# A Fourier-mixing and gated-MLP layer on one core: the first eight chunks alternate real and imaginary matrix, and four x tiles are normed on VectorE

## The chip, the core and the metric

One core of a Trainium2 chip runs the whole program in one launch. It has TensorE (PE: matmuls, with weight loads listed as PEld), VectorE (DVE), ScalarE (ACT), GpSimd (POOL) and SyncE (SP), which here only issues transfers. Each engine works through its own list of instructions strictly in the order in which the program wrote them, and waits on semaphores for the others. The metric is the time of one execution in microseconds (us). The kernel before takes 949.74 us, the median of three runs (949.63 to 949.95).

## The reference, cut to what matters

```
mod = (silu(c) @ w_mod).reshape(6, 512)      # sa, ca, ga, sb, cb, gb
h = layernorm(x) * (1 + ca) + sa             # x: 2048 x 512
a, b = h @ hid_re.T, h @ hid_im.T
x = x + ga * (seq_re @ a - seq_im @ b)       # seq_re, seq_im: 2048 x 2048
h = layernorm(x) * (1 + cb) + sb
z = gelu(h @ w_in)                           # 512 x 1792
z1, z2 = z[:, :896], layernorm(z[:, 896:])
x = x + gb * ((z1 * (w_sp @ z2 + b_sp)) @ w_out)
```

The change touches the front of the first Fourier part alone: the layernorm of x, and the products of the two 2048x2048 sequence matrices with it.

## The kernel before, in words

The kernel computes the Fourier part as (sequence matrix @ normed x) @ hidden matrix. All products are made from split operands: a number is cut into a high part in the fp32r type and a low part that holds the rest, and each product is three matmuls, high times high, high times low and low times high (`matmul3`, L93 to L97; `mm_a`, L425, for the first chunks). One matmul has a 128x128 stationary operand and a 128x512 moving one.

The sequence matrices are read in quarters of 512 output rows (t = 0 to 3). For a quarter, a **block** is 512x512 of the real matrix `cr` (j = 0) or the imaginary `ci` (j = 1), 1 MB, loaded by four transfers into a `stage` tile (L151 to L165; two such buffers). A block gives four **chunks** n: 128 columns of the block, transposed by DVE into half of a `t` tile (L176 one chunk, L216 two at once), high part `ah` on ACT (L245), low part `al` on DVE (L252). Chunk n is multiplied with tile s of the normed x: four groups of 128 hidden columns, twelve matmuls a chunk. There are four `ah` buffers, three `al` buffers and two `t` pairs, so a chunk can be made ready only a few chunks ahead of PE. For t = 0 the blocks come as cr, ci for rows of x 0 to 511, then cr, ci for the next 512, and so on: chunks 0 to 3 use cr with x tiles 0 to 3, chunks 4 to 7 use ci with the same tiles, chunks 8 to 11 use cr with x tiles 4 to 7.

An x tile is 128 rows. Its path is: statistics on DVE (`stats_first` L367 for tiles 0 to 3, `stats_x` L364 with L103 and L105 for 4 to 9), mean and 1/sqrt on POOL (L374 and L375, or L107, L108 and L115), normed tile `xn` on ACT (L119), high part `hh` on ACT (L412), low part `hl` on DVE (L417). Tiles 0 to 3 are loaded at the start, 64 KB or 128 KB a transfer, between the pieces of the first block; of block 0 the first 64 columns of each 128 come first. Each transfer is issued by SP or ACT, and eight completion semaphores go round: a transfer can be issued only when the eighth before it has landed.

The order is written out by hand. `at(n, f, ...)` puts a step behind chunk n's matmuls, and `prep(n)` runs ahead of them: it makes the low part of chunk n+2, the transposition of n+4 and n+5 and the high part of n+3. The lists at L897 to L949 set the steps for the start and for x tiles 4 to 15. Four throwaway matmuls (L329 to L333) stand at the front of PE's list.

Of the kernel before, what the change touches and what calls it, by code (L numbers as in the profile page):

```python
# [8 lines left out]
F32 = mybir.dt.float32  # L9
F32R = mybir.dt.float32r  # L10
# [9 lines left out]
def fnet_gmlp_kernel(  # L20
# [102 lines left out]
    def at(n, f, *a):  # L123
        fill.setdefault(n, []).append((f, a))
# [50 lines left out]
    def squares(dst, block, k):  # L175
        nc.vector.transpose(dst.rearrange("p (b i) -> p b i", i=32), block[:, :, 32 * k:32 * k + 32])  # L176
# [173 lines left out]
    def load_x(g, ks=range(4), engs=(nc.sync,)):  # L350

        if g not in XG:
            if g % 2:
                XG[g] = spool.tile([P, 4, D], F32, tag="x", bufs=1, name=f"x{g}")
            else:
                XG[g] = hpool.tile([P, 4, D], F32, tag="h12", bufs=1, name=f"x{g}")
        k0, k1 = ks[0], ks[-1] + 1
        v = x.rearrange("(g a k i) d -> g a i k d", g=NQ, a=4, i=32)
        for a in range(4):
            engs[a % len(engs)].dma_start(XG[g][32 * a:32 * a + 32, k0:k1, :], v[g, a][:, k0:k1, :])  # L360
        for k in ks:
            X[4 * g + k] = XG[g][:, k, :]
# [4 lines left out]
    def stats_first(s):  # L367

        m = spool.tile([P, 12], F32, tag="first", bufs=4, name=f"first{s}")
        nc.vector.bn_stats(m[:, :6], X[s])  # L370
# [53 lines left out]

    def mm_a(n):  # L425
        t, r = divmod(n, 8 * NQ)
        j, s = ((r // 4) % 2, r // 8 * 4 + r % 4) if t == 0 else (r // NS, r % NS)
        if s == 0:
            for k in range(ND):
                GP[t, j, k] = bank(4 * j + k if t == 0 else ring[0] % 6, f"gp{t}_{j}_{k}")  # L430
                ring[0] += t > 0
        ah, al = AH.pop(n), AL.pop(n)
        if n < 4:
            order = (h_hi[s], al), (h_lo[s], ah)
            for a, b in ((h_hi[s], ah),) + (order if n else order[::-1]):
                for k in range(ND):
                    nc.tensor.matmul(GP[0, 0, k], a[:, k, :], b, start=s == 0 and b is ah and a is h_hi[s], stop=False)
# [446 lines left out]


    both = (nc.sync, nc.scalar)
    load_x(0, range(1), both)
    stage[0] = blocks.tile([P, 16, P], F32, tag="stage", bufs=2, name="stage0")
    load_block(stage[0], src[0], 0, P // 2, both)
    load_x(0, range(1, 2), both)  # L890
    nc.scalar.activation(sc, ones[:, :ND], AF.Silu)
    load_x(0, range(2, 4))
    load_block(stage[0], src[0], P // 2, P)
    load(1)
    load_x(1, range(2))
    keep_busy(4, 5)
    for s in range(4):  # L897
        LN[s] = spool.tile([P, D], F32, tag="xn", bufs=4, name=f"xn{s}")
        nc.gpsimd.memset(LN[s][:, 0:1], 1.0)
    stats_first(0)  # L900
    norm_x(0)
    hi_h(0)
    turn_one(0)
    prep_hi(0, nc.vector)
    stats_first(1)
    lo_h(0)
    prep_lo(0)
    norm_x(1)
    hi_h(1)
    turn_one(1)  # L910
    prep_hi(1)
    stats_first(2)
    prep_lo(1)
    lo_h(1)
    norm_x(2)
    hi_h(2)
    turn_one(2)
    prep_hi(2)
    stats_first(3)
# [260 lines left out]
```

## Time and profile before

| what | value |
|---|---|
| median of three runs | 949.74 us |
| the profiled execution's own time | 950.4 us |
| its span on the core | 948.6 us |
| PE busy | 940.3 us (99%), 4160 matmuls |
| DVE busy | 704.5 us (74%) |
| ACT busy | 387.6 us (41%) |
| POOL busy | 175.5 us (19%) |
| granted TensorE clock, mean | 0.999 |
| moved by transfers | 161.25 MB, mean 170 GB/s |

A row of the timeline has the start in us from the start of the span, the duration in us, the engine, the line, the operation and the tiles that it writes and reads; "x4" merges four equal instructions, and the bracket names the idle time of the engine ahead of it and what ended it. A row of the waits has the total, the count and the longest. A row of the groups has the busy time and the mean duration in ns of one. A row of the windows has, for a stretch of the span, its length and each engine's busy time, then the granted clock, the share of the 16 transfer engines and the GB/s. The profile is one execution, 0.66 us above the median of the three runs.

### The profile page before, as it was taken

To read this page: it belongs to the slowest core of one execution; us is meant where nothing else is said; L and a number is where in the kernel's file an instruction comes from. 1 tells how busy PE (TensorE), PEld (TensorE's weight loads), DVE (VectorE), ACT (ScalarE), POOL (GpSimd) and SP (SyncE) were. 2 spreads that over 40 slices of the span, in tenths; PEclk is the share of its full clock that TensorE was granted. 3 is DMA by queue.
4 is the path that set the end of the run, shared out by engine and by line. 5 is a ranking of instruction groups with operands and counts; after the bars stand their busy time and mean duration, and the time that the engine had idled before them with its cause. 6 is when DMAs were issued, how large, how long until landed. Compare 5 with 4: busy or idle time off the path is not lost.

```text
span 948.6 us, 12279 instructions
## 1 busy us (share of the span) xinstructions
PE 940.3 (99%) x4160; PEld 780.9 (82%) x4160; DVE 704.5 (74%) x1039; ACT 387.6 (41%) x665; POOL 175.5 (19%) x331
## 2 busy tenths in 40 slices
PE   8999999999999999999999999999999999999998
PEld 5888888888888888888788999888888888888886
DVE  6799857775576666767978588877788688885872
ACT  4685424232132222322776456644544444331221
POOL 2431000121531144122432265200000000000000
PEclk9999999999999999999999999999999999999999
DMA  9997653676437965996596984555554455833551
GB/s 208 220 218 154 116 139 82 151 189 155 133 85 195 279 203 159 278 276 144 144 309 256 330 260 155 156 110 135 133 129 94 101 122 134 210 97 125 164 189 58
DMA packets 249230, 161.25 MB, mean 170 GB/s; under 512 B 130192, under 2 KB 218512, under 8 KB 249040
## 3 DMA queue, kind: packets, MB, share of 16 engines
q1 hardware_dynamic: 235792, 120.75, 52.8%
q0 software_dynamic: 11984, 39.07, 11.5%
q8 instruction: 32, 0.52, 0.2%
q10 hardware_dynamic: 1392, 0.66, 0.2%
q14 instruction: 30, 0.25, 0.1%
HBM read 123.73 MB, written 36.70 MB: 169 GB/s over the span
## 4 chain that ended last, share of the span: by engine, by line
PE 50%; DVE 1%; ACT 1%; POOL 1%; issue 0%; ACTq 0%; DVEq 0%; POOLq 0%
PE gw L96 10%; PE gw L95 10%; PE gw L97 10%; PE z2p L96 3%; PE z2p L97 3%; PE z2p L95 3%; PE op L97 3%; PE op L95 3%; PE op L96 3%; PE z1p L96 1%; PE z1p L95 1%; PE z1p L97 1%; PE z1g L95 1%; PE z1g L96 1%; PE z1g L97 1%
## 5 line engine op out<-in xcount | busy, mean ns | idle before, releaser
L245 ACT ACTIVATE ah<-t 128x512 fp32r<-128x512 f32 x263 | 164.4, 627 | 308.0 <-PE gp L97 183.3
L252 DVE TENSOR_TENSOR al<-t,ah 128x512 fp32r<-128x512 f32 x264 | 180.3, 686 | 141.7 <-PE gp L96 63.2
L96 PE MATMUL gp<-al,hh 128*128 128x512 f32 x496 | 193.1, 389 | 0.0
L95 PE MATMUL gp<-ah,hh 128*128 128x512 f32 x496 | 193.0, 389 | 0.0
L97 PE MATMUL gp<-ah,hl 128*128 128x512 f32 x496 | 193.0, 389 | 0.0
L97 PE MATMUL gw<-ah,bl 128*128 128x512 f32 x400 | 155.6, 389 | 0.0
L96 PE MATMUL gw<-al,bh 128*128 128x512 f32 x400 | 155.6, 389 | 0.0
L95 PE MATMUL gw<-ah,bh 128*128 128x512 f32 x400 | 155.6, 389 | 0.0
L96 PEld LDWEIGHTS gp<-al,hh 128*128 128x128 f32 x496 | 93.1, 188 | 19.7 <-DVE al L252 0.4
L95 PEld LDWEIGHTS gp<-ah,hh 128*128 128x128 f32 x496 | 93.1, 188 | 19.3
L97 PEld LDWEIGHTS gp<-ah,hl 128*128 128x128 f32 x496 | 93.1, 188 | 19.2
L97 PEld LDWEIGHTS gw<-ah,bl 128*128 128x128 f32 x400 | 75.1, 188 | 15.7
L95 PEld LDWEIGHTS gw<-ah,bh 128*128 128x128 f32 x400 | 75.1, 188 | 15.7
L96 PEld LDWEIGHTS gw<-al,bh 128*128 128x128 f32 x400 | 75.1, 188 | 15.4
L216 DVE STREAM_TRANSPOSE t<-stage 128x1024 f32<-128x1024 f32 x64 | 79.3, 1239 | 7.0 <-DMA stage<-in_A_dft_seq_re_dram 6.0
L210 DVE STREAM_TRANSPOSE t<-stage 128x1024 f32<-128x1024 f32 x56 | 69.4, 1239 | 0.1
L751 ACT ACTIVATE bh<-z 128x512 fp32r<-128x512 f32 (+1 forms) x56 | 32.8, 587 | 66.2 <-PE gw L96 66.2
L729 POOL DMA_DIRECT2D s_d<-sj x64 | 35.1, 550 | 109.2 <-DVE sj L721 64.7
L95 PE MATMUL yp<-hth,gh 128*128 128x512 f32 x128 | 49.8, 389 | 0.0
L96 PE MATMUL yp<-htl,gh 128*128 128x512 f32 x128 | 49.8, 389 | 0.0
L97 PE MATMUL yp<-hth,gl 128*128 128x512 f32 x128 | 49.8, 389 | 0.0
L96 PE MATMUL z2p<-wil,ah 128*128 128x448 f32 x128 | 46.7, 365 | 0.0
(204 smaller groups left out, 1420.4 us busy)
## 6 DMA issues: line engine op xcount, KB each, us to landing
stage<-in_A_dft_seq_im_dram SPq DMA_DIRECT2D x64, 256.0 KB, 5.6
sj<-in_B_w_sp_dram SPq DMA_DIRECT2D x32, 512.0 KB, 8.2
s_d<-sj POOLq DMA_DIRECT2D x64, 256.0 KB, 4.3
stage<-s_d SPq DMA_DIRECT2D x128, 128.0 KB, 2.8
stage<-in_A_dft_seq_re_dram SPq DMA_DIRECT2D x60, 256.0 KB, 5.4
stage<-in_B_w_sp_dram SPq DMA_DIRECT2D x96, 128.0 KB, 3.1
stage<-h_d SPq DMA_DIRECT2D x32, 256.0 KB, 6.2
wm<-in_w_mod_dram SPq DMA_DIRECT2D x16, 256.0 KB, 4.8
```

The costliest lines, as they stand in the source:

```text
L95: nc.tensor.matmul(acc, ah, bh, start=first, stop=False, skip_group_check=go_on)
L96: nc.tensor.matmul(acc, ah, bl, start=False, stop=False, skip_group_check=go_on)
L97: nc.tensor.matmul(acc, al, bh, start=False, stop=last, skip_group_check=go_on)
L210: nc.vector.transpose(t.rearrange("p r (b i) -> p r b i", i=32), st[:, :, :, 16 * k:16 * k + 32])
L216: nc.vector.transpose(t.rearrange("p k (b i) -> p k b i", i=32), st[:, :, 32 * k:32 * k + 64].rearrange("p b (k i) -> p k b i", k=2))
L245: nc.scalar.activation(AH[n], source(n), AF.Copy)
L252: nc.vector.tensor_tensor(AL[n], source(n), AH[n].bitcast(F32), op=ALU.subtract)
L729: nc.gpsimd.dma_start(s_d[m, r, g][b * P:(b + 1) * P, :], a)
L751: nc.scalar.activation(BH[p, k][:, :w], b_of(p, k), AF.Copy)
```

## The change

Five things change, all at the start.

1. Chunks 0 to 7 alternate: chunk n uses block n % 2 (cr or ci) and x tile n // 2. So x tile s serves chunks 2s and 2s + 1. `mm_a` writes all eight in the groups' order that only the first four had, and `turn_one` transposes one chunk at a time for all eight.
2. The loads at the front are reordered: x tile 0 in two transfers (SP and ACT) instead of four; then the first half of block 0 and the first half of block 1, each in four transfers by two issuers; then x tiles 1 and 2, the second halves of both blocks, x tile 3. Block 2 gets a buffer of its own (that of `wb`) and is loaded ahead of x tiles 4 to 7.
3. Rows 0 to 3 of x tiles (x tiles 0 to 3) are normed on DVE, (x - mean) * rstd in one tensor_scalar and a memset of one column (`norm_first`); POOL does one step (the power) instead of two, and ACT none.
4. Chunk 0 is transposed in two halves of 256; the high part of the first half is made by ACT, that of the second by DVE.
5. The steps for x tiles 4 and 5 are written into a new list: statistics of tile 4 behind chunk 4, its norm, high and low part and then the statistics of tile 5 behind chunk 5, and the rest of tile 5 behind chunk 6. Tiles 6 and up keep their places.

```diff
-    def turn_one(n):
-        squares(slot(n), stage[n // 4], n % 4)
+    def turn_one(n, b0=0, b1=16):
+        if b0 == 0:
+            slot(n)
+        squares(T[n][:, 32 * b0:32 * b1], stage[n % 2][:, b0:b1], n // 2)
...
-        nc.gpsimd.tensor_scalar(mv[:, 3:4], mv[:, 0:1], mv[:, 2:3], -1.0, op0=ALU.mult, op1=ALU.mult)
-        NRM[s] = mv[:, 2:3], mv[:, 3:4]
+        NRM[s] = mv[:, 0:1], mv[:, 2:3]
...
-        j, s = ((r // 4) % 2, r // 8 * 4 + r % 4) if t == 0 else (r // NS, r % NS)
+        j, s = (r % 2, r // 2) if n < 8 else ((r // 4) % 2, r // 8 * 4 + r % 4) if t == 0 else (r // NS, r % NS)
...
-        if n < 4:
+        if n < 8:
...
-            for a, b in ((h_hi[s], ah),) + (order if n else order[::-1]):
+            for a, b in ((h_hi[s], ah),) + (order if j == 0 else order[::-1]):
...
+    def load_row_tile(s):
+        v = x[:Q].rearrange("(a k i) d -> k a i d", a=4, i=32)[s]
+        for i in range(2 if s == 0 else 1):
+            o = slice(2 * i, 2 * i + 2) if s == 0 else slice(0, 4)
+            both[i].dma_start(XG[0][32 * o.start:32 * o.stop, s, :], v[o])
+    load_row_tile(0)
+    load_block(stage[0], src[0], 0, P // 2, both)
+    load_block(stage[1], src[1], 0, P // 2, both)
+    load_row_tile(1)
...
+    load_block(stage[2], src[2])
+    load_x(1, range(2))
...
+    def norm_first(s):
+        m = NRM.pop(s)
+        nc.vector.tensor_scalar(LN[s], X.pop(s), m[0], m[1], op0=ALU.subtract, op1=ALU.mult)
+        nc.vector.memset(LN[s][:, 0:1], 1.0)
...
+                     (4, (stats_x, 4), (prep_lo, 7), (turn_two, 8)),
+                     (5, (norm_x, 4), (hi_h, 4), (lo_h, 4), (stats_x, 5)),
+                     (6, (norm_x, 5), (hi_h, 5), (lo_h, 5))):
...
-    for s, n in ((4, 4), (5, 4), (6, 6), (7, 6), (8, 10), (9, 10)):
+    for s, n in ((6, 6), (7, 6), (8, 10), (9, 10)):
```

Line numbers of the changed kernel stand 7 higher from `turn_two` on, 6 higher behind `stats_first`, and 37 higher behind the start. Three places show how the instructions move.

DVE's list from the first statistics on, before (`first` holds an x tile's statistics, x0 the x tiles 0 to 3, t0 chunks 0 and 1):

```order
L370 BN_STATS first0_178<-x0_132 128x6
L372 BN_AGGR first0_178<-first0_178 128x2
L373 TENSOR_SCALAR first0_178<-first0_178 128x1
L176 STREAM_TRANSPOSE t0_187<-stage0_137 128x512
L243 TENSOR_SCALAR ah0_189<-t0_187 128x512
L370 BN_STATS first1_191<-x0_132 128x6
L372 BN_AGGR first1_191<-first1_191 128x2
L373 TENSOR_SCALAR first1_191<-first1_191 128x1
L417 TENSOR_TENSOR hl0_197<-xn0_170,hh0_185 128x512
```

And the same place now:

```order
L377 BN_STATS first0_172<-x0_134 128x6
L379 BN_AGGR first0_172<-first0_172 128x2
L380 TENSOR_SCALAR first0_172<-first0_172 128x1
L924 TENSOR_SCALAR xn0_177<-x0_134,first0_172 128x512
L925 MEMSET xn0_177 128x1
L176 STREAM_TRANSPOSE t0_182<-stage0_132 128x256 x2
L933 TENSOR_SCALAR ah0_184<-t0_182 128x256
L259 TENSOR_TENSOR al0_188<-t0_182,ah0_184 128x512
L423 TENSOR_TENSOR hl0_190<-xn0_177,hh0_180 128x512
```

The norm of tile 0 has come in ahead of the transposition, which is now two halves, and the statistics of tile 1 have gone behind both low parts and the transposition of chunk 1.

DVE's list around the work for chunks 8 and 9, before (bstx and mvx are statistics of x tiles 5, 6 and 7 in turn, x1 the x tiles 4 to 7, hl4 and hl5 the low parts of x tiles 4 and 5, al7 to al9 those of chunks 7 to 9):

```order
L103 BN_STATS bstx_364<-x1_160 128x6
L105 BN_AGGR mvx_366<-bstx_364 128x2
L252 TENSOR_TENSOR al7_373<-t6_288,ah7_332 128x512
L252 TENSOR_TENSOR al8_400<-t8_330,ah8_375 128x512
L216 STREAM_TRANSPOSE t10_402<-stage2_236 128x1024
L103 BN_STATS bstx_427<-x1_160 128x6
L105 BN_AGGR mvx_429<-bstx_427 128x2
L103 BN_STATS bstx_436<-x1_160 128x6
L105 BN_AGGR mvx_438<-bstx_436 128x2
L252 TENSOR_TENSOR al9_445<-t8_330,ah9_409 128x512
L417 TENSOR_TENSOR hl4_461<-xn4_394,hh4_423 128x512
L417 TENSOR_TENSOR hl5_463<-xn5_397,hh5_425 128x512
```

And the same place now (the statistics of tile 4 and al7 stand just ahead of it):

```order
L223 STREAM_TRANSPOSE t8_356<-stage2_157 128x1024
L423 TENSOR_TENSOR hl4_382<-xn4_377,hh4_380 128x512
L103 BN_STATS bstx_384<-x1_162 128x6
L105 BN_AGGR mvx_386<-bstx_384 128x2
L259 TENSOR_TENSOR al8_398<-t8_356,ah8_363 128x512
L223 STREAM_TRANSPOSE t10_400<-stage2_157 128x1024
L423 TENSOR_TENSOR hl5_426<-xn5_421,hh5_424 128x512
L103 BN_STATS bstx_428<-x1_162 128x6
L105 BN_AGGR mvx_430<-bstx_428 128x2
L103 BN_STATS bstx_437<-x1_162 128x6
L105 BN_AGGR mvx_439<-bstx_437 128x2
L259 TENSOR_TENSOR al9_446<-t8_356,ah9_407 128x512
```

The low parts hl4 and hl5, which stood behind all statistics of tiles 4 to 7 and behind al9, now stand ahead of the statistics of tile 5 and of tiles 6 and 7; al8 and al9 stand behind them.

SP's list of transfers from the start, before (stage0 is the first cr block, stage1 the first ci block, stage2 the second cr block; 32x16x64 is a quarter of half a block):

```order
L360 DMA x0_132<-in_A_x_dram 32x512 x2
L154 DMA stage0_137<-in_A_dft_seq_re_dram 32x16x64 x2
L360 DMA x0_132<-in_A_x_dram 32x512 x2
L360 DMA x0_132<-in_A_x_dram 32x2x512 x4
L154 DMA stage0_137<-in_A_dft_seq_re_dram 32x16x64 x4
L154 DMA stage1_155<-in_A_dft_seq_im_dram 32x16x128 x4
L360 DMA x1_160<-in_A_x_dram 32x2x512 x4
L154 DMA stage2_236<-in_A_dft_seq_re_dram 32x16x128 x4
L360 DMA x1_160<-in_A_x_dram 32x2x512 x4
```

And now:

```order
L901 DMA x0_134<-in_A_x_dram 64x1x512
L154 DMA stage0_132<-in_A_dft_seq_re_dram 32x16x64 x2
L154 DMA stage1_133<-in_A_dft_seq_im_dram 32x16x64 x2
L901 DMA x0_134<-in_A_x_dram 128x1x512 x2
L154 DMA stage0_132<-in_A_dft_seq_re_dram 32x16x64 x4
L154 DMA stage1_133<-in_A_dft_seq_im_dram 32x16x64 x4
L901 DMA x0_134<-in_A_x_dram 128x1x512
L154 DMA stage2_157<-in_A_dft_seq_re_dram 32x16x128 x4
L367 DMA x1_162<-in_A_x_dram 32x2x512 x8
```

Half of block 1 has come in ahead of x tile 1, all of it in half-width pieces, and stage2 ahead of x tiles 4 to 7.

More of the change, by code (lines that the diff above doesn't have):

```diff
@@ L196, in slot @@
         return T[n]
[L198 to L199 removed]
+    def turn_one(n, b0=0, b1=16):
+        if b0 == 0:
+            slot(n)
+        squares(T[n][:, 32 * b0:32 * b1], stage[n % 2][:, b0:b1], n // 2)
+        if n // 2 == 3 and b1 == 16:
+            stage.pop(n % 2)
+            if n % 2:
+                load(3)
     def turn_two(n):
@@ L886, in fnet_gmlp_kernel @@
     both = (nc.sync, nc.scalar)
-    load_x(0, range(1), both)
-    stage[0] = blocks.tile([P, 16, P], F32, tag="stage", bufs=2, name="stage0")
+    def load_row_tile(s):
+        if 0 not in XG:
+            XG[0] = hpool.tile([P, 4, D], F32, tag="h12", bufs=1, name="x0")
+        v = x[:Q].rearrange("(a k i) d -> k a i d", a=4, i=32)[s]
+        for i in range(2 if s == 0 else 1):
+            o = slice(2 * i, 2 * i + 2) if s == 0 else slice(0, 4)
+            both[i].dma_start(XG[0][32 * o.start:32 * o.stop, s, :], v[o])
+        X[s] = XG[0][:, s, :]
@@ L889, in fnet_gmlp_kernel @@
+    for b in range(2):
+        stage[b] = blocks.tile([P, 16, P], F32, tag="stage", bufs=2, name=f"stage{b}")
+    load_row_tile(0)
     load_block(stage[0], src[0], 0, P // 2, both)
-    load_x(0, range(1, 2), both)
+    load_block(stage[1], src[1], 0, P // 2, both)
+    load_row_tile(1)
     nc.scalar.activation(sc, ones[:, :ND], AF.Silu)
-    load_x(0, range(2, 4))
+    load_row_tile(2)
     load_block(stage[0], src[0], P // 2, P)
-    load(1)
+    load_block(stage[1], src[1], P // 2, P)
+    load_row_tile(3)
@@ L895, in fnet_gmlp_kernel, with hi_half @@
+    stage[2] = spool.tile([P, 16, P], F32, tag="wb", bufs=1, name="stage2")
+    load_block(stage[2], src[2])
     load_x(1, range(2))
     keep_busy(4, 5)
-    for s in range(4):
+    def norm_first(s):
         LN[s] = spool.tile([P, D], F32, tag="xn", bufs=4, name=f"xn{s}")
-        nc.gpsimd.memset(LN[s][:, 0:1], 1.0)
+        m = NRM.pop(s)
+        nc.vector.tensor_scalar(LN[s], X.pop(s), m[0], m[1], op0=ALU.subtract, op1=ALU.mult)
+        nc.vector.memset(LN[s][:, 0:1], 1.0)
+    def hi_half(n, b0, b1, eng=None):
+        if b0 == 0:
+            split_done.add((n, 0))
+            AH[n] = blocks.tile([P, Q], F32R, tag="ah", bufs=4, name=f"ah{n}")
+        c = slice(32 * b0, 32 * b1)
+        if eng:
+            eng.tensor_scalar(AH[n][:, c], T[n][:, c], 1.0, None, op0=ALU.mult)
+        else:
+            nc.scalar.activation(AH[n][:, c], T[n][:, c], AF.Copy)
```

41 lines of the change are left out of this document (19 added, 22 removed).

## The prediction

> **What bounds the kernel now.** First the page's busy times, then PE's waits in the first 40 us, then the timeline there.
>
> ```profile
> PE 940.3 (99%) x4160; PEld 780.9 (82%) x4160; DVE 704.5 (74%) x1039; ACT 387.6 (41%) x665; POOL 175.5 (19%) x331
> ...
> PE gp L437 <- ACT ah L245: 1.1, 2, 0.7
> PE gp L437 <- DVE ah L243: 1.0, 1, 1.0
> PE gp L437 <- DVE hl L417: 0.4, 1, 0.4
> ```
>
> PE is busy for 99% of the span, so a change can win only where PE waits, or lose by making it wait. Three of the waits are at the front, and these rows show how they end.
>
> ```profile
> 0.73 0.87 SPq L360 DMA_DIRECT2D x<-in_A_x_dram  x2
> 1.65 0.95 SPq L154 DMA_DIRECT2D stage<-in_A_dft_seq_re_dram  x2
> 3.90 0.69 DVE L370 BATCH_NORM_STATS2 first<-x 128x6 f32<-128x512 f32 x1 [2.51 <-DMA x<-in_A_x_dram]
> 6.82 0.71 DVE L176 STREAM_TRANSPOSE t<-stage 128x512 f32<-128x512 f32 x1 [1.82 <-DMA stage<-in_A_dft_seq_re_dram]
> 7.56 0.43 DVE L243 TENSOR_SCALAR ah<-t 128x512 fp32r<-128x512 f32 x1
> 8.13 1.17 PE L437 MATMUL gp<-ah,hh 128*128 128x512 f32 x4 [1.04 <-DVE ah L243]
> ...
> 21.62 0.39 PE L95 MATMUL gp<-ah,hh 128*128 128x512 f32 x1
> 32.51 0.39 PE L95 MATMUL gp<-ah,hh 128*128 128x512 f32 x1
> 51.95 0.50 PE L96 MATMUL gp<-al,hh 128*128 128x512 f32 x1
> 52.28 0.40 PE L97 MATMUL gp<-ah,hl 128*128 128x512 f32 x1
> 54.60 0.39 PE L95 MATMUL gp<-ah,hh 128*128 128x512 f32 x1
> ```
>
> Chunk 0 starts at 8.13, behind the landing of the block (6.82). Chunk 4 starts at 21.62 and chunk 8 at 32.51: 10.89 us for four chunks, 2.72 a chunk or 0.227 a matmul, with no waiting. Chunks 0 to 3 take 13.49, so 2.6 go to waits; chunk 16 at 54.60 is 22.09 behind chunk 8, 0.3 more than eight chunks need (the step at 51.95). After a wait the first step is 0.33 (51.95 to 52.28), 0.1 over the usual.
>
> DVE is what makes the first chunks slow; its own pace between two of its operations:
>
> ```profile
> 14.29 0.65 DVE L370 BATCH_NORM_STATS2 first<-x 128x6 f32<-128x512 f32 x1
> 15.27 0.70 DVE L176 STREAM_TRANSPOSE t<-stage 128x512 f32<-128x512 f32 x1
> 15.89 0.66 DVE L252 TENSOR_TENSOR al<-t,ah 128x512 fp32r<-128x512 f32 x1
> 16.47 0.68 DVE L417 TENSOR_TENSOR hl<-xn,hh 128x512 fp32r<-128x512 f32 x1
> ...
> L216 DVE STREAM_TRANSPOSE t<-stage 128x1024 f32<-128x1024 f32 x64 | 79.3, 1239 | 7.0 <-DMA stage<-in_A_dft_seq_re_dram 6.0 <-DMA stage<-in_A_dft_seq_im_dram 0.9
> L480 DVE TENSOR_SCALAR acc<-ht,col 128x512 f32<-128x512 f32 x2 | 1.0, 481 | 0.0
> ```
>
> From start to start, the statistics of an x tile cost 0.98 with their small steps, a transposition 0.62, a low part 0.58 to 0.6. A chunk that brings an x tile needs 0.98 + 0.62 + 2 x 0.59 = 2.8 of DVE, over PE's 2.72.
>
> **The start, part by part.** Each queue now issues one x transfer ahead of the block instead of two, 0.87 / 2 = 0.43 us sooner, so I put the landing at 6.82 - 0.43 = 6.4; if the landing is set by bytes and not by the issue, nothing is won. The norm of tile 0 on DVE replaces ACT's and one POOL step; the nearest row is L480, 0.48, plus a memset of one column of about 0.1. It ends near 6.1, in the 1.82 us that DVE waited ahead of 6.82, so it is covered. Two half transpositions: 1239 - 710 ns for 512 more columns leaves 0.18 fixed, so 0.44 each, the second 0.36 behind the first. DVE's half of the high part takes between half of 0.43 and all of it; I take 0.29, by the half with some fixed part. Together 0.36 + 0.44 + 0.03 + 0.29 = 1.12 against 7.99 - 6.82 = 1.17: the halves win 0.05 at most, and lose 0.1 at the upper end. PE starts at 6.4 + 1.12 + 0.14 = 7.65 instead of 8.13.
>
> Then an x tile serves two chunks. A pair costs DVE two transpositions, two al, one hl, the statistics, the norm and its memset: 1.24 + 1.18 + 0.59 + 0.98 + 0.6 = 4.6, and about 0.2 in which al waits for an ah that ACT makes from a transposition only two operations ahead. 4.8 is under PE's 5.44. So the 2.6 us of waits nearly go; I leave 0.3 for chunks 1 and 2, whose block half and x tile land late. Chunk 8 would start at 7.65 + 0.3 + 8 x 2.72 = 29.7 instead of 32.51: a lead of 2.8. POOL's shorter work and ACT's freed time are off the path.
>
> **What is late next.** Chunks 8 to 11 need x tiles 4 to 7. Before, their statistics ran in twos, well ahead:
>
> ```profile
> 24.67 1.25 DVE L216 STREAM_TRANSPOSE t<-stage 128x1024 f32<-128x1024 f32 x1 [1.39 <-DMA stage<-in_A_dft_seq_re_dram]
> 25.84 0.65 DVE L103 BATCH_NORM_STATS2 bstx<-x 128x6 f32<-128x512 f32 x1
> 26.52 0.18 DVE L105 BATCH_NORM_AGGREGATE mvx<-bstx 128x2 f32<-128x6 f32 x1
> 26.62 0.66 DVE L103 BATCH_NORM_STATS2 bstx<-x 128x6 f32<-128x512 f32 x1
> 27.07 0.55 POOL L108 TENSOR_TENSOR rsx<-mvx,mhalf 128x1 f32<-128x1 f32 x1
> 27.42 1.27 DVE L252 TENSOR_TENSOR al<-t,ah 128x512 fp32r<-128x512 f32 x2
> 27.72 1.02 POOL L115 TENSOR_SCALAR nmrx<-mvx,rsx 128x1 f32<-128x1 f32 x1
> 28.78 0.81 ACT L119 ACTIVATE xn<-x,nmrx,rsx 128x511 f32<-128x511 f32 x1 [2.12 <-POOL nmrx L115]
> 28.83 0.19 POOL L107 TENSOR_SCALAR mvx<-mvx 128x1 f32<-128x1 f32 x1
> 29.75 0.27 POOL L115 TENSOR_SCALAR nmrx<-mvx,rsx 128x1 f32<-128x1 f32 x1
> 31.30 1.14 ACT L412 ACTIVATE hh<-xn 128x512 fp32r<-128x512 f32 x2
> ```
>
> A tile's way from statistics to high part is long: 0.68 to the second DVE step, then 1.5 by POOL's quick set (0.28 to its start as from 26.52, 28.83 to 30.02) or 2.26 by the slow one (26.52 to 28.78), 0.81 for xn, 0.6 for hh. Before, two tiles went through it side by side. Now DVE's list has hl4 ahead of the statistics of tile 5, and hl5 ahead of those of tiles 6 and 7; hl4 and hl5 wait for ACT, so DVE stands still in each tile's way, and al8, al9, the transposition t10 and the next statistics are queued behind them. I walk through it.
>
> When do tile 4's statistics start? By DVE: tile 1's wait for its transfer. These windows give the bytes:
>
> ```profile
> 0.00:8.10 8.10, 5.56 (x8) 2.22 (x8) 2.77 (x7) 2.93 (x4) 1.39 (x12) 1.00 0.63 172
> 8.10:12.40 4.30, 3.28 (x12) 2.09 (x12) 3.58 (x9) 1.95 (x3) 1.71 (x3) 1.00 0.97 233
> ```
>
> 1.39 MB by 8.10; x tile 1 ends 1.57 MB of the new order, 0.8 us later, and some 0.6 for landing: 9.5. Three pairs on: 9.5 + 14.4 = 23.9. By transfers: x tile 4 now lands behind block 2, and what must have landed is the same 4.5 MB (x tiles 0 to 5, three blocks) as for the transposition at 24.67. I take the later one, 24.7.
>
> Tile 4's statistics 24.7, al7 25.5, t8 26.1 to 27.35, ah8 on ACT 27.4, xn4 27.9, hh4 28.7 to 29.3, hl4 29.35, tile 5's statistics 29.95, aggregate 30.65, al8 30.75 to 31.45. Chunk 8's second matmul needs al8 and is due at 29.9: it starts at 31.55, **1.6 late**. POOL is done with tile 5 between 32.15 and 32.9, say 32.5; xn5 to 33.3, hh5 to 33.95, hl5 34.0, tiles 6 and 7 statistics 34.6 and 35.4, al9 36.2 to 36.9. Chunk 9's second matmul is due at 31.55 + 12 x 0.227 = 34.3 and starts at 37.0: **2.7 late**. POOL then needs two sets for tiles 6 and 7, 1.2 to 1.95 each from 35.6, so 38.0 to 39.5, say 38.5; ACT's list has xn7 and ah11 ahead of hh6: xn7 38.5, ah11 39.2, hh6 39.75 to 40.35. Chunk 10 is due at 39.6 and starts at 40.4, **0.8 late**; its third matmul waits for hl6, behind al11, until 41.25, **0.3 late**. Behind that tiles 6 and 7 are ready and the old spacing returns.
>
> Sum: 5.4 of waits, 0.4 for four restarts, less the lead of 2.8: chunk 11 starts 3.0 later than before. The 0.3 lost ahead of chunk 16 is a wait for data that come no later than now, so it goes: 2.7 net. From there PE has no slack to make it up. 950.4 + 2.7 = 953.1 for a profiled execution; this one stands 0.66 over the median, so **952.4**.
>
> The slow and the quick POOL set are the term with the widest ends. Both rows above show it: L115 took 1.02 while DVE ran two low parts (27.42 to 28.69), 0.27 at 29.75 beside statistics. The Trainium skill, page "SBUF — State Buffer", section "SBUF: two separate sides", says that DVE with two SBUF inputs and a GpSimd operation that reads SBUF hold a shared port exclusively, the later one blocking for the whole instruction. The trace agrees (1.02 against 0.27). By that rule tile 6's last POOL step would wait out al9 and al10, to about 37.5, and tile 7's end near 38.8: 0.3 over my sum.
>
> **Rivals.**
> Faster: the three gaps are covered, because DVE comes to tile 4 early enough. Then chunk 11 keeps the lead, and with the 0.3 the time is 950.4 - 3.1 - 0.66 = 946.6. It decides at al9: 12.2 us lie between tile 4's statistics and al9's end, and al9 is due at 29.7 + 2.95 = 32.65, so the statistics would have to start by 20.4. DVE's 4.6 a pair and the 24.67 row speak against that. 0.08.
>
> Quick chain: POOL's quick sets (0.35 for tile 5, 0.5 for tiles 6 and 7) and DVE's 23.9 instead of 24.7 take 1.7 off: 950.7, within 0.2%. 0.2.
>
> Later data: half-width pieces of block 1 cost transfer time that the equal bytes hide; tile 4's statistics at 26 and slow POOL sets add 1.3 + 0.4 + 0.6: 954.7. 0.07.
>
> Cold clock: a gap of 2.7 in PE brings back the pace at which it started:
>
> ```profile
> 4.23 0.34 PEld L333 LDWEIGHTS busyp<-busy,ones 128*128 128x128 f32 x1 [0.52 <-issue]
> 5.08 0.32 PEld L333 LDWEIGHTS busyp<-busy,ones 128*128 128x128 f32 x1 [0.52 <-issue]
> 5.65 0.19 PEld L333 LDWEIGHTS busyp<-busy,ones 128*128 128x128 f32 x1 [0.24 <-issue]
> 6.08 0.19 PEld L333 LDWEIGHTS busyp<-busy,ones 128*128 128x128 f32 x1 [0.24 <-issue]
> ```
>
> 0.85 a step until about 5.3, then 0.43: half speed for 3.7 us from 1.5 on. Once more, that costs half of it, 1.8: 954.2. The waits behind 8.13, 0.7 at most in the rows above, did not do this. 0.05. The Trainium skill, page "TensorE: Matmul & The Clock Gate", section "What's actually happening", has the half rate return after an idle window of about 3.4 us; by it a 2.7 gap would cost nothing.
>
> **The numbers.** Forecast 952.4, its own range 951.2 to 954.0, 0.6. From the bounds (1.8 less, 2.5 more) the range is 950.6 to 954.9. A measurement here can tell 0.2%, 1.9 us. Faster 0.08; within 0.2%: the quick chain and the forecast's lower edge, 0.23; slower 0.69.
>
> **What would show it.** PE's first gp matmul near 7.65 and chunk 8 near 29.7 for the lead; then PE waiting for DVE al by 1.6 and 2.7 and for ACT hh between 30 and 41, DVE idle ahead of hl on ACT, the clock at 1.00. It is wrong if PE runs through 30 to 41 without such waits, or if tile 4's statistics start before 21.

## The result: 967.55 us, and the profile after

The changed kernel takes 967.55 us (median of 5, 966.63 to 968.02) against 949.78 (949.63 to 949.95) for the kernel before: a ratio of 1.0186, 95% interval 1.0175 to 1.0198. That is 17.8 us slower, where 2.6 were forecast (952.4, range 950.6 to 954.9). The profiled execution took 967.55 with a span of 965.8, and its span is 17.2 over the span before; the profiled execution of before stood 0.66 above its median, which is the rest of the 17.8.

The page's busy row and PE's waits of the changed kernel:

```profile
PE 946.4 (98%) x4160; PEld 784.5 (81%) x4160; DVE 707.2 (73%) x1050; ACT 385.4 (40%) x662; POOL 171.7 (18%) x323
...
PE gp L443 <- DVE ah L933: 6.9, 1, 6.9
PE gp L95 <- ACT hh L418: 3.1, 2, 2.1
PE gp L96 <- DVE al L259: 1.6, 1, 1.6
...
PE gp L443 <- DVE al L259: 1.1, 1, 1.1
```

PE is busy for 6 more than before and idle for 11 more. Of the forecast waits, the 1.6 for al at chunk 8 is there (1.63) and the 0.8 for hh at chunk 10 too (1.02). The 2.7 for al at chunk 9 is not, since PE runs at half rate and comes there later; in its place chunk 8 waits 2.13 for the high part of its x tile. The 6.9 for the first high part is new, and so is the added busy time. The timeline (start, length, engine, line, operation; in brackets the idle time ahead and what ended it) shows the first, and the others in their order:

```profile
0.73 1.14 ACTq L901 DMA_DIRECT2D x<-in_A_x_dram  x1
0.73 0.72 SPq L901 DMA_DIRECT2D x<-in_A_x_dram  x1
...
2.70 8.11 SPq L154 DMA_DIRECT2D stage<-in_A_dft_seq_im_dram  x2
2.84 6.17 ACTq L154 DMA_DIRECT2D stage<-in_A_dft_seq_im_dram  x2
...
10.58 0.69 DVE L377 BATCH_NORM_STATS2 first<-x 128x6 f32<-128x512 f32 x1 [9.19 <-DMA x<-in_A_x_dram]
...
14.44 2.05 PE L443 MATMUL gp<-ah,hh 128*128 128x512 f32 x4 [6.90 <-DVE ah L933]
16.28 1.91 PE L443 MATMUL gp<-al,hh 128*128 128x512 f32 x4
...
17.77 0.69 DVE L377 BATCH_NORM_STATS2 first<-x 128x6 f32<-128x512 f32 x1 [1.46 <-DMA x<-in_A_x_dram]
...
30.38 0.69 DVE L377 BATCH_NORM_STATS2 first<-x 128x6 f32<-128x512 f32 x1 [2.75 <-DMA x<-in_A_x_dram]
...
38.01 0.69 DVE L103 BATCH_NORM_STATS2 bstx<-x 128x6 f32<-128x512 f32 x1 [2.60 <-DMA x<-in_A_x_dram]
...
43.31 0.49 PE L95 MATMUL gp<-ah,hh 128*128 128x512 f32 x1 [2.13 <-ACT hh L418]
45.43 0.80 PE L96 MATMUL gp<-al,hh 128*128 128x512 f32 x1 [1.63 <-DVE al L259]
46.03 0.63 PE L97 MATMUL gp<-ah,hl 128*128 128x512 f32 x1
46.45 0.63 PE L95 MATMUL gp<-ah,hh 128*128 128x512 f32 x1
```

The first statistics are the key row: 10.58 instead of 3.90. x tile 0 was issued at 0.73, as before, and its statistics could run only 9.8 us later. Tiles 1 and 3 make DVE wait for x too; tile 4's statistics come at 38.01, where 24.7 was forecast. Twice PE then runs at 0.43 a matmul instead of 0.227: four matmuls lie between 14.44 and 16.28 (the first with 0.1 for its start), and 46.03 to 46.45 is one. The queues stand still as well: a pair of issues takes SP 8.11 and ACT 6.17. A transfer can be issued only when the eighth before it has landed, and for the second issue of each pair that is one of x tile 0: SP waits 3.5 us for x there, against 0.3 in the version with four transfers below.

These windows of one us each give, after the busy times of the engines, the granted clock, the share of the 16 DMA engines that was busy (over 1 where more than 16 packets were in flight), and the GB/s:

```profile
4.00:5.00 1.00, 1.00 (x2) 0.34 (x1) 0.00 (x0) 0.00 (x0) 0.00 (x0) 1.00 1.27 275
...
6.00:7.00 1.00, 1.00 (x4) 0.47 (x2) 0.00 (x0) 0.00 (x0) 0.00 (x0) 1.00 0.17 52
7.00:8.00 1.00, 0.54 (x2) 0.00 (x0) 0.00 (x0) 0.00 (x0) 0.00 (x0) 1.00 0.27 84
...
13.00:14.00 1.00, 0.00 (x0) 0.00 (x0) 0.83 (x3) 0.86 (x2) 0.00 (x0) 0.50 0.21 52
```

275 GB/s at 4 to 5, and then 52 to 84 in the windows shown, with 0.17 to 0.27 of 16 engines busy: about 3 to 4 engines work while everybody waits for bytes. The five windows from 8 to 13 that are left out have 74 to 122 GB/s. 275 GB/s were to be had just before. This suggested the theory of the experiments: a transfer whose outermost count is 2 (tile 0: `v[o]` is [2, 32, 512]) or 4 (tiles 1 to 3) is carried by that many engines only. The Trainium skill, page "DMA: Bandwidth & Descriptors", section "Why a DMA increments its semaphore by 16 and not by 1", states such a rule: the number of engines is the largest one up to 16 that divides the slowest dimension of both access patterns. The experiments below agree with its order and, by the packets in flight, with its numbers of engines, but not with a time in proportion to them.

### The profile page after: what moved, and what is told of

Read it like the earlier page. It is cut to its first block, busy times and chain, and to the rows that moved or that the text cites. A ratio compares the mean times of both kernels' runs of the same rounds, so it can differ in the third digit from the quotient of the medians.

```text
span 965.8 us, 12265 instructions
## 1 busy us (share of the span) xinstructions
PE 946.4 (98%) x4160; PEld 784.5 (81%) x4160; DVE 707.2 (73%) x1050; ACT 385.4 (40%) x662; POOL 171.7 (18%) x323
## 4 chain that ended last, share of the span: by engine, by line
PE 50%; DVE 1%; ACT 1%; POOL 1%; issue 0%; ACTq 0%; DVEq 0%; POOLq 0%
PE gw L96 9%; PE gw L95 9%; PE gw L97 9%; PE z2p L97 3%; PE z2p L96 3%; PE z2p L95 3%; PE op L95 3%; PE op L96 3%; PE op L97 3%; PE z1p L96 1%; PE z1p L97 1%; PE z1p L95 1%; PE z1g L95 1%; PE z1g L96 1%; PE z1g L97 1%
## 5 line engine op out<-in xcount | busy, mean ns | idle before, releaser
L95 PE MATMUL gp<-ah,hh 128*128 128x512 f32 x480 | 187.8, 391 | 3.1 <-ACT hh L418 3.1
L96 PE MATMUL gp<-al,hh 128*128 128x512 f32 x480 | 188.0, 392 | 1.8 <-DVE al L259 1.6
L97 PE MATMUL gp<-ah,hl 128*128 128x512 f32 x480 | 187.8, 391 | 0.1
L95 PEld LDWEIGHTS gp<-ah,hh 128*128 128x128 f32 x480 | 90.7, 189 | 22.9 <-ACT hh L418 4.0
L96 PEld LDWEIGHTS gp<-al,hh 128*128 128x128 f32 x480 | 90.6, 189 | 21.4 <-DVE al L259 2.7
L97 PEld LDWEIGHTS gp<-ah,hl 128*128 128x128 f32 x480 | 90.6, 189 | 19.4 <-DVE hl L423 0.5
L223 DVE STREAM_TRANSPOSE t<-stage 128x1024 f32<-128x1024 f32 x62 | 76.7, 1238 | 0.0
L217 DVE STREAM_TRANSPOSE t<-stage 128x1024 f32<-128x1024 f32 x56 | 69.3, 1238 | 0.2
```

What stands on the lines that cost most here:

```text
L95: nc.tensor.matmul(acc, ah, bh, start=first, stop=False, skip_group_check=go_on)
L96: nc.tensor.matmul(acc, ah, bl, start=False, stop=False, skip_group_check=go_on)
L97: nc.tensor.matmul(acc, al, bh, start=False, stop=last, skip_group_check=go_on)
L217: nc.vector.transpose(t.rearrange("p r (b i) -> p r b i", i=32), st[:, :, :, 16 * k:16 * k + 32])
L223: nc.vector.transpose(t.rearrange("p k (b i) -> p k b i", i=32), st[:, :, 32 * k:32 * k + 64].rearrange("p b (k i) -> p k b i", k=2))
```

## Experiments

Times are medians; the kernel before took 949.6 to 949.8 beside each.

**Four transfers of 32 rows for each of tiles 0 to 3.** The shape of the kernel before, all else as changed:

```diff
-        for i in range(2 if s == 0 else 1):
-            o = slice(2 * i, 2 * i + 2) if s == 0 else slice(0, 4)
-            both[i].dma_start(XG[0][32 * o.start:32 * o.stop, s, :], v[o])
+        for a in range(4):
+            (both[a % 2] if s == 0 else nc.sync).dma_start(XG[0][32 * a:32 * a + 32, s, :], v[a])
```

> The changed kernel, but each of x tiles 0 to 3 comes in four transfers of 32 rows (tile 0's in turn from both queues), as in the kernel before. Main theory: a transfer whose outer count is 2 (tile 0) or 4 (tiles 1 to 3) is served by that many of the 16 engines, so tile 0 lands at about 10 instead of 3.7, and what is queued behind it is late too. Then here tile 0 lands by 4, its statistics run at about 3.9 as in the kernel before, PE's first gp matmul is near 8, the clock is 1.00 there, and the time falls from 967.6 to what was forecast for the rest of the change, 951 to 955. Rival, order: the halves of block 1 and the single-queue tiles are what holds x and the blocks up; then PE still starts after 11 and the time stays over 960. Rival, chain: the serial way of x tiles 4 to 7 costs far more than the 2.7 forecast; then PE starts near 8 and the time still is over 957.

Measured: 954.53, ratio 1.0050 (1.0035 to 1.0065). Its timeline:

```profile
3.80 0.70 DVE L377 BATCH_NORM_STATS2 first<-x 128x6 f32<-128x512 f32 x1 [2.41 <-DMA x<-in_A_x_dram]
...
6.27 0.06 DVE L924 MEMSET xn<- 128x1 f32 x1
6.41 0.77 DVE L176 STREAM_TRANSPOSE t<-stage 128x256 f32<-128x256 f32 x2
...
7.70 1.48 PE L443 MATMUL gp<-ah,hh 128*128 128x512 f32 x4
...
14.27 0.65 DVE L377 BATCH_NORM_STATS2 first<-x 128x6 f32<-128x512 f32 x1
...
19.19 0.65 DVE L377 BATCH_NORM_STATS2 first<-x 128x6 f32<-128x512 f32 x1
...
25.32 0.69 DVE L103 BATCH_NORM_STATS2 bstx<-x 128x6 f32<-128x512 f32 x1 [1.12 <-DMA x<-in_A_x_dram]
...
30.20 0.50 PE L95 MATMUL gp<-ah,hh 128*128 128x512 f32 x1 [0.16 <-ACT hh L418]
32.32 0.50 PE L96 MATMUL gp<-al,hh 128*128 128x512 f32 x1 [1.62 <-DVE al L259]
...
37.86 0.50 PE L96 MATMUL gp<-al,hh 128*128 128x512 f32 x1 [2.42 <-DVE al L259]
38.20 0.46 PE L97 MATMUL gp<-ah,hl 128*128 128x512 f32 x1
38.46 0.63 PE L95 MATMUL gp<-ah,hh 128*128 128x512 f32 x1
...
41.45 0.57 PE L96 MATMUL gp<-al,hh 128*128 128x512 f32 x1
41.86 0.40 PE L97 MATMUL gp<-ah,hl 128*128 128x512 f32 x1
```

13.0 of the 17.8 us are the shape of the x transfers. What is left is the forecast kernel: PE at 7.70, a pair of chunks in 4.9 of DVE (14.27 to 19.19), waits of 1.62 and 2.42. Tile 4's statistics are at 25.32 here and 12.69 later in the changed kernel, nearly the whole 13.0.

**As many transfers, of consecutive rows.** This separates the shape from the number, which stays at two for tile 0 and one for each other.

```diff
-        v = x[:Q].rearrange("(a k i) d -> k a i d", a=4, i=32)[s]
...
-            both[i].dma_start(XG[0][32 * o.start:32 * o.stop, s, :], v[o])
+        n = 2 if s == 0 else 1
+        for i in range(n):
+            o = slice(P // n * i, P // n * (i + 1))
+            both[i].dma_start(XG[0][o, s, :], x[P * s + o.start:P * s + o.stop, :])
```

> The changed kernel with as many transfers from the same queues (two for x tile 0, one for each of tiles 1 to 3), but each takes 64 or 128 consecutive rows of x, so its outer count is 64 or 128. It reads other rows than the kernel before, so the output is another one; bytes, order and number of transfers are those of the changed kernel. Main theory (the outer count sets the number of engines): tile 0 lands by about 4, PE starts near 7.7, the time is 951 to 955, within 1 of the version with four transfers. Rival, number: two large transfers in place of four small ones are slow by themselves; then PE starts after 11 and the time stays over 960.

Measured: 953.90, PE's first matmul at 7.92. The rival, number, falls. PE's waits at chunks 8 to 10, from the timeline:

```profile
31.74 0.50 PE L96 MATMUL gp<-al,hh 128*128 128x512 f32 x1 [1.52 <-DVE al L259]
...
37.28 0.50 PE L96 MATMUL gp<-al,hh 128*128 128x512 f32 x1 [2.42 <-DVE al L259]
...
41.09 0.51 PE L95 MATMUL gp<-ah,hh 128*128 128x512 f32 x1 [0.97 <-ACT hh L418]
```

All three forecast waits are there, and no half rate in this profile, where that of the version with four transfers had half rate and no third wait.

**The two shapes apart.** Tile 0 alone in four transfers:

```diff
-        for i in range(2 if s == 0 else 1):
-            o = slice(2 * i, 2 * i + 2) if s == 0 else slice(0, 4)
-            both[i].dma_start(XG[0][32 * o.start:32 * o.stop, s, :], v[o])
+        if s == 0:
+            for a in range(4):
+                both[a % 2].dma_start(XG[0][32 * a:32 * a + 32, s, :], v[a])
+        else:
+            nc.sync.dma_start(XG[0][:, s, :], v)
```

> The changed kernel with x tile 0 alone in four transfers of 32 rows; tiles 1 to 3 keep their single transfers with an outer count of 4. Main theory: tile 0 lands by 4 and PE starts near 8, but 256 KB on four engines at some 3 to 6 KB a us each per engine take 10 us or more, and tile 1's statistics come near 15 instead of 11: chunks 2, 4 and 6 are late, PE stops for 2 to 5 us, and the time is 954 to 962. If tiles 1 to 3 do no harm, it equals the version with all four tiles mended, within 1. Rival, order: over 960 with PE's start after 11.

Measured: 960.57, PE at 7.60, tile 1's statistics at 11.93 and not near 15. No run shows the 3 to 6 KB a us for each engine that the expectation took; by the packets of this trace, a row of 2 KB takes 84 ns (median) and four are in flight at a time between 8 and 11. And tiles 1 to 3 alone:

```diff
-        for i in range(2 if s == 0 else 1):
-            o = slice(2 * i, 2 * i + 2) if s == 0 else slice(0, 4)
-            both[i].dma_start(XG[0][32 * o.start:32 * o.stop, s, :], v[o])
+        if s == 0:
+            for i in range(2):
+                both[i].dma_start(XG[0][64 * i:64 * i + 64, s, :], v[2 * i:2 * i + 2])
+        else:
+            for a in range(4):
+                nc.sync.dma_start(XG[0][32 * a:32 * a + 32, s, :], v[a])
```

> The changed kernel with x tiles 1 to 3 in four transfers of 32 rows each, and tile 0 as it was, in two of [2, 32, 512]. The converse (tile 0 mended alone) gave 960.6, both mended 954.5, none 967.6. Main theory (each transfer of a small outer count holds a few of the 16 engines, and what comes behind it in issue order waits): tile 0 again lands at 8.5 to 10.5, its statistics run at about 10.5, PE starts at 14 to 14.5 at half rate; the tiles behind it are then late by no more than tile 0 itself, 6.5, so the time is 958 to 961.5. If the two harms were one (tile 0's late issue alone holds up the rest), the time stays at 965 to 968; if only tiles 1 to 3 count, it is 954 to 956.

Measured: 960.08, PE at 14.28. So tile 0's shape costs 5.6 by itself, tiles 1 to 3's cost 6.0, both 13.0: two harms that add up, with 1.4 more together. Tile 4's statistics stood at 31.46 and 30.93.

**The kernel before with tile 0 in two transfers.**

```diff
-    load_x(0, range(1), both)
+    XG[0] = hpool.tile([P, 4, D], F32, tag="h12", bufs=1, name="x0")
+    v = x[:Q].rearrange("(a k i) d -> k a i d", a=4, i=32)[0]
+    for i in range(2):
+        both[i].dma_start(XG[0][64 * i:64 * i + 64, 0, :], v[2 * i:2 * i + 2])
+    X[0] = XG[0][:, 0, :]
```

> The kernel before with one part of the change alone: x tile 0 in two transfers of [2, 32, 512], one from each queue. Main theory: it lands near 9 to 10 instead of 3.7, PE's first gp matmul moves from 8.1 to about 12 to 14, PE runs at half rate for some us behind that gap, and the time rises by 5 to 9, to 955 to 959. Rival, order or chain: fewer transfers are issued 0.4 sooner and nothing else changes: 949 to 950.

Measured: 955.68 (ratio 1.0062, 1.0047 to 1.0077), first statistics at 10.30, PE at 14.05. The one line that looked like a saving of 0.43 costs 5.9 us in the old kernel too.

**How much by the outer count.** The kernel before with tile 0 in a single transfer of 256 KB from SP. With a count of 4, beside the version above:

```diff
-    for i in range(2):
-        both[i].dma_start(XG[0][64 * i:64 * i + 64, 0, :], v[2 * i:2 * i + 2])
+    nc.sync.dma_start(XG[0][:, 0, :], v)
```

> The kernel before with x tile 0 in one transfer of [4, 32, 512] from one queue: 256 KB as in the run with two transfers of [2, 32, 512], with an outer count of 4 instead of 2. Main theory (the outer count is the number of engines): twice the engines carry the same bytes, so tile 0 lands at about 6 to 7 instead of 10, PE's first gp matmul is at 10 to 11.5 instead of 14, with no or a short half rate, and the time is 950 to 952.5 (two transfers: 955.7). Rival, bytes or number of transfers: one transfer of 256 KB from one queue is as late or later than two of 128 KB from two, 955 to 959.

Measured: 953.55, over the 950 to 952.5 expected and under the rival's 955; PE at 11.84. For counts G of 2, 8 and 16:

```diff
-    v = x[:Q].rearrange("(a k i) d -> k a i d", a=4, i=32)[0]
+    v = x[:Q].rearrange("(g r) d -> g r d", g=G)[:, :128 // G]
```

> The kernel before with x tile 0 in one transfer of 256 KB from SP whose outer count is 2 ([2, 64, 512]; it reads other rows of x, so the output is another one; bytes and packets are the same). With an outer count of 4 the first statistics ran at 8.1 (issue at 0.7, first bytes at about 2.4). Theory, outer count is the number of engines: 128 KB an engine instead of 64, so the transfer takes twice as long, and the first statistics run at 12 to 14. Rival, the single queue or the size of the transfer sets it: at 8 again, whatever the count.

> As the run with an outer count of 2, but with 8 ([8, 16, 512]). Theory: 32 KB an engine, half the time of the run with 4: the first statistics at 5 to 5.7. Rival: at 8 again.

> As the run with an outer count of 2, but with 16 ([16, 8, 512]). Theory: 16 KB an engine, a quarter of the time of the run with 4: the first statistics at 3.7 to 4.4, as early as with four transfers of 32 rows (3.9). Rival: at 8 again, or later, if many pieces with gaps between them are slow.

The first statistics with a count of 2:

```profile
10.19 0.69 DVE L370 BATCH_NORM_STATS2 first<-x 128x6 f32<-128x512 f32 x1 [8.80 <-DMA x<-in_A_x_dram]
```

Of 4:

```profile
8.09 0.69 DVE L370 BATCH_NORM_STATS2 first<-x 128x6 f32<-128x512 f32 x1 [6.70 <-DMA x<-in_A_x_dram]
```

Of 8:

```profile
5.80 0.69 DVE L370 BATCH_NORM_STATS2 first<-x 128x6 f32<-128x512 f32 x1 [4.41 <-DMA x<-in_A_x_dram]
```

Of 16:

```profile
4.85 0.69 DVE L370 BATCH_NORM_STATS2 first<-x 128x6 f32<-128x512 f32 x1 [3.46 <-DMA x<-in_A_x_dram]
```

Same bytes, same queue, same number of transfers: 10.19, 8.09, 5.80, 4.85. The rival of one time for all falls. But my sizes were off, each outside its range: half the count never doubled the time. The single executions with 2, 8 and 16 took 956.67, 951.02 and 950.62.

So the order is shown, and the traces have the number of engines as well: they list each packet with its start, length and size, and at the front only rows of x are packets of 2 KB. At the start of the transfer as many of them are in flight as its count says: 2 with a count of 2 (2.6 to 3.3 us), 4 with 4 (2.6 to 3.5), 8 with 8 (3 to 4), 15 with 16 (3 to 3.5). In the changed kernel the 128 rows of tile 0 run from 2.2 to 10.0, two in flight for both transfers together and not two for each; at 115 ns a row on average that makes 7.4 us of it. In the version with four transfers 15 are in flight, and the rows are through by 3.1.

**Throwaway matmuls** in the changed kernel:

```diff
-    keep_busy(4, 5)
+    keep_busy(20, 5)
```

> The changed kernel as it is (2 and 4 engines for the x tiles), with 20 throwaway matmuls ahead of the first gp matmul instead of 4, so that PE is busy until about 14 and never idle for 6.9. Theory, clock: the half rate between 14.4 and 19.7 comes from PE's idle time alone; then PE starts at about 14.4 to 15 at full rate, and the time falls by 2.0 to 2.8 from 967.6, to 964.8 to 965.6. If the half rate has another cause, or if what the half rate loses was waited for anyway, the time stays within 1 of 967.6.

Measured: 967.83. I had sized it badly: 20 of them kept PE until 20.9, 6.5 past the former start. It answers nonetheless: PE started 6.5 later, at full clock, and the time is the same. Tile 4's statistics are at 38.18 (38.01 without the edit), and the waits for al behind them are 1.63 and 2.42. In the changed kernel neither the late start of PE nor its half rate until 19.7 costs anything by itself; the loss is set further on, where chunks 8 to 11 wait for tile 4 and those behind it.

**x tiles 4 and 5 ahead of block 2**, in the version with four transfers:

```diff
+    load_x(1, range(2))
     load_block(stage[2], src[2])
-    load_x(1, range(2))
```

> The version with tiles 0 to 3 in four transfers each (954.5), with one edit more: x tiles 4 and 5 are loaded ahead of block 2 and not behind it. There tile 4's statistics waited 1.1 for x, which landed at 25.2 with DVE free since 24.2; DVE's list is left as it is. Main theory (the serial way of tiles 4 to 7 through POOL and ACT makes the waits of 1.9 and 2.7 at chunks 8 and 9): the whole row starts about 1.1 earlier, the first wait shrinks to 0.8 to 1.2, the second stays at 2.4 to 2.9, and the time is 952 to 954, less if the gaps no longer bring the half clock back. Rival, data: the waits follow from x tiles and block 2 landing late; then both waits nearly go and the time is under 950.

Measured: 953.24 (1.0025 to 1.0050), PE's waits at chunks 8 and 9 are 1.2 and 2.4, then 1.0 for hh. The row moved up by 1.0 (chunk 9's second matmul at 36.87, 37.86 without the edit), its waits stayed: data were a part of it, 1.3 us.

**Another list for tiles 4 to 7**, in that version:

```diff
-                     (3, (norm_first, 3), (hi_h, 3), (prep_lo, 6), (lo_h, 3), (turn_one, 7), (prep_hi, 7)),
-                     (4, (stats_x, 4), (prep_lo, 7), (turn_two, 8)),
-                     (5, (norm_x, 4), (hi_h, 4), (lo_h, 4), (stats_x, 5)),
-                     (6, (norm_x, 5), (hi_h, 5), (lo_h, 5))):
+                     (3, (norm_first, 3), (hi_h, 3), (prep_lo, 6), (lo_h, 3), (stats_x, 4), (stats_x, 5), (turn_one, 7), (prep_hi, 7)),
+                     (4, (norm_x, 4), (hi_h, 4), (prep_lo, 7), (turn_two, 8)),
+                     (5, (lo_h, 4), (prep_lo, 8), (norm_x, 5), (prep_hi, 9), (hi_h, 5), (stats_x, 6), (stats_x, 7),
+                      (prep_lo, 9), (lo_h, 5)),
+                     (6, (norm_x, 6)),
+                     (7, (hi_h, 6), (prep_lo, 10), (lo_h, 6), (norm_x, 7), (hi_h, 7)),
+                     (8, (prep_lo, 11), (lo_h, 7))):
...
-    for s, n in ((6, 6), (7, 6), (8, 10), (9, 10)):
+    for s, n in ((8, 10), (9, 10)):
```

> As the version with the loads of x tiles 4 and 5 ahead of block 2, and with another list for tiles 4 to 7: the statistics of 4 and 5 stand together ahead of the transposition of chunk 7, those of 6 and 7 behind the low part of chunk 8, and no low part of h stands on DVE ahead of statistics that another tile waits for. Main theory (serial chain): the waits at chunks 8 to 10 fall from 5 to under 1, the clock stays at 1.00, the lead of 2.7 at chunk 8 is kept, and the time is 947 to 949, below the kernel before (949.8). Rival: the waits are DVE's and ACT's amount of work at this place and not its order; then some 3 to 5 of waits stay and the time is over 950.5.

Measured: 950.33 (1.0001 to 1.0019; single executions from 949.25 to 952.98). Of the waits at chunks 8 to 11 about 0.6 is left: it was the order, not the amount of work. The time is still above the expected 949, for a reason neither theory had. Its timeline:

```profile
48.52 1.25 DVE L223 STREAM_TRANSPOSE t<-stage 128x1024 f32<-128x1024 f32 x1 [5.52 <-DMA stage<-in_A_dft_seq_re_dram]
49.69 0.67 DVE L176 STREAM_TRANSPOSE wt<-wb 128x512 f32<-128x512 f32 x1
50.39 0.69 DVE L324 TENSOR_TENSOR wt<-wt,crow 128x512 f32<-128x512 f32 x1
51.00 0.68 DVE L259 TENSOR_TENSOR al<-t,ah 128x512 fp32r<-128x512 f32 x1
...
49.33 0.39 PE L95 MATMUL gp<-ah,hh 128*128 128x512 f32 x1
51.74 0.50 PE L96 MATMUL gp<-al,hh 128*128 128x512 f32 x1 [2.02 <-DVE al L259]
```

PE came to chunk 15 2.2 ahead of the kernel before and stood for al15, which DVE makes at 51.00, behind the transposition of block 4. That block lands when it did before (48.5; 48.7 there), since the transfers are no faster. In the kernel before the same queue cost 0.3, the wait that the prediction let go. This profiled execution took 951.81, and PE ran at half rate from 52.8 to 56.2, behind the wait of 2.02. Its mean granted clock is 0.998, as in the three others that took 951.8 or more; the seven with 0.999 or 1.000 took 949.25 to 950.58.

**al15 ahead of block 4's transposition**, `prep` leaving that one to the list:

```diff
-            if n % 2 == 0 and n and not N2 + 4 <= n + 4 < N3:
+            if n % 2 == 0 and n and n != 12 and not N2 + 4 <= n + 4 < N3:
...
+                     (12, (prep_lo, 15), (turn_two, 16))):
```

> As the version with the new list for tiles 4 to 7 (950.3), with one edit more: the low part of chunk 15 stands ahead of the transposition of block 4 on DVE, not behind it. There PE kept its lead of 2.2 over the kernel before until chunk 15, then waited 2.4 for that low part, which stood behind the transposition, and this waited 5.5 for the block's landing at 48.4, as late as before (48.6). Theory, queue: the block is early enough for chunk 16 itself, only the low part queued behind it is not; then the wait goes, the clock stays at 1.00, the lead is kept, and the time is 946.8 to 948. Rival, data: the block's landing bounds chunk 16 too, and the next blocks land as late as before whatever PE's lead; then the lead is lost one place further on, and the time is 949 to 950.5.

Measured: 949.32, ratio 0.9993 (0.9984 to 1.0002). The wait of 2.02 went, as the queue theory had it, but waits of 0.30 and 0.66 for low parts further on came in its place, and the time is in the rival's range. Next, **the first two column weightings behind the low parts of chunks 16 and 17**:

```diff
+                     (14, (prep_lo, 17))):
...
-    for j, ns in ((1, (12, 14, 17, 18)), (0, (21, 22, 23, 24))):
+    for j, ns in ((1, (14, 15, 17, 18)), (0, (21, 22, 23, 24))):
```

> As the version with the low part of chunk 15 ahead of the transposition of block 4 (949.3), with two edits more in the same place: the first two column weightings (a transposition and a product of 128x512 each on DVE, 1.3 together) stand behind the low parts of chunks 16 and 17, not ahead of them. There PE's lead of 2.5 over the kernel before at chunk 16 fell to 0.9 by chunk 18, in waits of 0.5 and 0.8 for DVE's low parts. Theory, queue: these waits are what stands ahead of the low parts on DVE, so at least 0.8 of the lost 1.6 comes back, and the time is 947.4 to 948.6, the first version below the kernel before (949.75) by more than 0.1%. Rival, data: the blocks behind block 4 land when they land, and the lead falls to 0.9 a chunk or two later anyway: 949 to 949.6.

Measured: 949.13, ratio 0.9993 (0.9984 to 1.0002). One wait of 0.7 is left, ahead of the matmul at 58.4. Here too the rival has the time: the lead is lost a place further on. A lead of 2.7 at chunk 8 ends as 0.4 to 0.6 us, too little to be told from the kernel before. What lands too late behind block 4 was not followed further.

**The first high part in one piece**, in the version with four transfers:

```diff
-    turn_one(0, 0, 8)
-    hi_half(0, 0, 8)
-    turn_one(0, 8, 16)
-    hi_half(0, 8, 16, nc.vector)
+    turn_one(0)
+    prep_hi(0, nc.vector)
```

> The version with tiles 0 to 3 in four transfers each (954.5, PE's first gp matmul at 7.70), with the first transposition and the first high part whole, on DVE, as in the kernel before, not in halves on two engines. The forecast put the halves at a gain of 0.05 at most, because two short operations cost more than one and the chain from the transposition to PE is 1.12 against 1.17: the start moves by 0.1 at most (7.7 to 7.85) and the time stays within 0.5 of 954.5. Rival: the halves are worth 0.3 or more, and the first matmul is at 8.0 or later.

Measured: 954.45, PE at 7.81. The versions with halves start between 7.60 and 7.92: no difference.

## Why the prediction was wrong

1. *The step that failed*: "Each queue now issues one x transfer ahead of the block instead of two, 0.87 / 2 = 0.43 us sooner, so I put the landing at 6.82 - 0.43 = 6.4." I priced the transfers by their number and bytes, never by their shape. The norm of tile 0, which I had end near 6.1 and covered by the landing of the block, ended at 13.1, because tile 0's rows came two at a time until 10.0; chunk 0's transposition went right behind it (13.20), and no longer behind the block. The same slip stands in the landing of tile 1 (9.5 from the bytes of the windows; its statistics ran at 17.77). The runs put the shape at 13.0 us: 5.6 for tile 0, 6.0 for tiles 1 to 3, 1.4 for both together. No rival named it; "later data" went that way with the wrong reason and 2 us.
2. *The start without that*: right in size, PE at 7.70 against 7.65 with the shape mended, but by luck in part. What releases the transposition (6.41) is the end of the norm (6.33) and not the landing put at 6.4: DVE does not wait for the block there. Nor was an earlier issue seen to win anything: the version of consecutive rows has one x transfer a queue ahead of the block and started at 7.92. The halves are worth nothing, as said.
3. *Two chunks for a tile*: right. 4.9 of DVE a pair (14.27 to 19.19) against 4.8; chunk 8 started at 30.20 behind a wait of 0.16, at 29.82 in the version of consecutive rows, against 29.7.
4. *The serial way of tiles 4 to 7*: right in place and size. Waits of 1.6, 2.7 and 0.8 were forecast, 1.52, 2.42 and 0.97 came in the version of consecutive rows. Tile 4's statistics were at 25.32 against 24.7, held by x tile 4 behind block 2, which I had named and taken 0.6 too early; in the version of consecutive rows they ran at 24.37 with no wait for data. (The 4.5 MB of that step are 4.7 in the unit of its 1.57; the row it is set beside has the same bytes.) The new list removes these waits, so order is the cause.
5. *The sum*: the rest of the change was to cost 2.6 and costs 4.7 (954.53 against 949.83). 0.7 of this is the 0.66 that I took off, since the profiled execution of before stood above its median: 954.39 for the profiled one here is no such outlier. About 1.2 are lag in the trace: chunk 16 starts at 58.50, 3.9 behind the 54.60 of before, where 2.7 were forecast. 0.6 of the 1.2 come from tile 4's later statistics, for the version of consecutive rows, which has them sooner, is 0.6 ahead from chunk 9's second matmul on (37.28 against 37.86). The other 0.6 it has too: 0.3 by that matmul (37.0 forecast), and 0.4 more at chunk 10 (41.09, 40.4 forecast).
6. *Cold clock*: given 0.05 and 1.8, it came: 3.4 us at half rate behind the 2.42 wait. But it cost nothing there: the version that kept its clock is 0.58 ahead before it (37.28 against 37.86) and 0.60 behind it (chunk 11 at 44.30 against 44.90), because the wait for hh that follows (0.97) and the short ones behind it were swallowed. In the changed kernel the first half rate cost nothing either. With the new list, where no such wait follows, the executions with the lower clock took about 2 longer.
7. *Faster, 946.6*: would not have come even with all three gaps covered. The version that covers them gave 950.3, because "a wait for data that come no later than now" holds only for a kernel that is late; one that is early meets that wait in full.

## What to carry to other kernels

Before merging transfers, write down the outermost count of both access patterns: with four transfers of 32 rows the first statistics run more than 6 us sooner here than with two of [2, 32, 512], though the last two are issued later. A stretch with few GB/s and a low share of DMA engines, while engines wait for bytes, is the sign to look for. In this kernel a lead at the front was worth only what the next queued wait for data left of it: look for operations queued behind a transposition that waits for a block.

## What the runs showed of the hardware that was not expected

- A transfer on few engines holds up what is issued behind it: mending tiles 1 to 3 alone moved tile 4's statistics from 38.01 to 30.93.
- Two transfers with an outer count of 2, issued on two queues, shared two engines: two rows were in flight for both, and they landed as late (10.30, in the kernel before) as one transfer of the same bytes with that count (10.19).
- The half rate lasted from 38.46 to 41.86 behind a wait of 2.42, and came after 0.6 at full rate (37.86 to 38.46). A wait of the same 2.42 in the profiled execution of the version of consecutive rows brought none, and with the new list only some executions have the lower clock. The Trainium skill, page "TensorE: Matmul & The Clock Gate", section "What's actually happening", has windows of about 3.4 us that run free of the kernel; the 3.4 agrees. By that, whether a gap is punished depends on where it falls, and my reading that one of 2.7 costs nothing was wrong: gaps of 2.42 and 2.02, shorter than such a window, brought the half rate.
